# Where the splits of the first weights stand in a planned instruction order, and how long the plan takes conversions to be

## The chip, the cores and the metric

The kernel runs on one core of one Trainium2 chip. The metric is the device time of the whole program in microseconds (us); 1018.32 us is the median of three runs before the change. Five engines matter: TensorE (PE, matrix products; PEld is its weight load), VectorE (DVE), ScalarE (ACT), GpSimd (POOL) and SyncE (SP), which issues all transfers (DMA).

## The reference, in short

2304 tokens (4 batches of 576) pass through three layers in turn:

- attention of 8 heads of 64 columns, masked by blocks of 64 positions: `softmax(q k^T / 8) v`, with the row's maximum taken off before the exponential;
- a first feed-forward layer: `h = x @ w_in`, `g = max(0.01 h, h)`, `y = g @ w_out`, with 512 columns in and out and 2048 between;
- a second one of the same size with `g = h * sigmoid(h)`.

The weights come in as 64-bit floats and are turned into 32-bit floats on the chip.

## The kernel before

**Blocks.** The first two layers run over six blocks of 384 tokens (blocks 0 to 5), the third over nine blocks of 256 tokens. While PE runs the feed-forward steps of block b, the attention of block b+1 runs beside them on DVE, ACT, POOL and in between on PE. One step f (of 16) of a block is a first product with 128 of the 2048 columns (`first_layer`, lines 1114 to 1121), the gate on ACT (L1167), and a second product into four accumulators (`second_layer`, L1131 or L1139). Step (1, 0) is the first step of block 1.

**Precision.** Block 0's feed-forward steps multiply the 32-bit weights as they are (L1114, L1131). All later blocks multiply parts: a weight w is *split* into hi (w rounded to the type that PE takes at full rate) and lo = w - hi. Each half of a step's weights (128 x 512) is one ACT copy (L296) and one subtraction (L312) on DVE or POOL; with 16 steps and two halves each that is 32 copies and 32 subtractions, tile `w` in the trace. Step (1, f) cannot start before its splits are there.

**Conversion.** `convert` turns 128 x 512 weights from 64 to 32 bits: a load, a scaling on ACT (L344), the low word on DVE (L354) or ACT (L352), the sign on DVE (L357), a shift on DVE (L361), and an integer addition on DVE or POOL (L366). It serves the first weights (32 conversions, while block 0 runs) and the second weights (32 conversions, from about 470 us on).

**Where splits go.** The split of the first five steps and of one more half goes into tiles that the start of block 0 leaves; the next ones need the tiles of block 1's keys (free when the last scores of block 1 are done); from the middle of step 8 on they go into the tiles of block 0's own weights.

**Attention.** A unit is 128 queries of a head: scores on PE (L838; L833 for block 1), their maximum on DVE (L847, L850), the exponential on ACT (L855), the normalised probabilities in two parts (L869 or L871, L874), a transposing DMA (L882), and the products with the values on PE (L896 to L898), then two small operations that gather a head's rows (L721, L727). Block 2 has 24 units. When all heads are there, `x` of the block is split in two (tiles xhi, xlo), and the block's first step can start.

**The order.** Nothing is ordered at run time. `Schedule.run` (L84) simulates the engines once, when the program is built: each task has a length per engine that may take it, the tasks it needs, and a rank. An engine that is free takes the waiting task of lowest rank; if a task may go to two engines, the second one is offered it 450 ns later and with the rank raised by 14. What comes out is the order of instructions on each engine, and the chip keeps to it. A length marked `Both` also waits for the port that DVE and POOL share in the plan.

**The ranks.** Gates have rank -1000 and more, scores and value products -500; a step (b, f) of the feed-forward layers has 16 b + f. Conversions of first weights have 10.5 + 0.7 f (10.5 to 21), block 1's attention 11 to 12.6. Block 2's units have 79 to 91.8 in order, and the preparation of their keys and queries stands 4 lower, from 75 on. The splits of step f have `step_of(1, f) - LEAD` and one more for every second half:

```
ts = split(DM, lambda d=d: d["x"], parts, deps, step_of(1, f) - LEAD + i % 2, [last] if last else [])
```

With LEAD = 2.0 that is 14 to 30.

Of the kernel before, what the change touches and what calls it, by code (L numbers as in the profile page):

```python
# [29 lines left out]
LATE = 10  # L30
NATIVE = 15
WARM = 11
LEAD = 2.0
LOAD0 = -1000
TURN = 0
COLD = 1.2
# [176 lines left out]
def attn_mlp_mlp(  # L213
# [13 lines left out]
    NT, DM = out.shape  # L227
# [33 lines left out]
    plan = Schedule()  # L261


    def act(n, psum=False, pointers=0):
        return 0.833 * n + (52 if psum else 94) + 93 * pointers

    def dve(n, pointers=0):
        return Both(1.042 * n + 68 + 61 * pointers)
# [4 lines left out]
    def dve2x(n, pointers=0):  # L273
        return Both(0.521 * n + 68 + 61 * pointers)

    def pool(n):
        return Both(2.35 * n + 100)
# [10 lines left out]
    def dma(deps, rank, size, emit, issue=600, after=()):  # L288
        t = plan.add({"SP": issue}, deps, rank, lambda e: emit(), after)
        done = plan.add({"DMA": size / 360}, [t], rank, lambda e: None)  # L290
        done.issue = t
        return done
# [13 lines left out]
    def on_vector(n):  # L306
        return {"DVE": dve(n), "POOL": pool(n)}
# [9 lines left out]
    def step_of(blk, f):  # L317
        return blk * NF + f
# [7 lines left out]
    def convert(src, f, sl, rk, load_rank, to=None):  # L326

        d = {}  # L330
        raw_free, raw_after, raw_users = raws.next()
        cy_free, cy_after, cy_users = cys.next()
        cc_free, cc_after, cc_users = ccs.next()

        def load():
            r = raw.tile([P, DM], I64, tag="wraw", name="wraw")
            nc.sync.dma_start(out=r, in_=src[f, :, sl])
            d["w0"] = r.bitcast(U32).rearrange("p (n two) -> p n two", two=2)[:, :, 0]
            d["sign"] = r.bitcast(U16).rearrange("p (n four) -> p n four", four=4)[:, :, 3]
            d["top"] = r.bitcast(F32).rearrange("p (n two) -> p n two", two=2)[:, :, 1]  # L340

        def scaled(e):
            d["y"] = cy.tile([P, DM], F32, tag="cy", name="cy")
            nc.scalar.activation(d["y"], d["top"], AF.Copy, scale=2.0**-112)  # L344

        def half_words(i):
            return d["c"].bitcast(U16).rearrange("p (n two) -> p n two", two=2)[:, :, i]

        def low(e):
            d["c"] = cc.tile([P, DM], U32, tag="cc", name="cc")  # L350
            if e == "ACT":
                nc.scalar.activation(half_words(0), d["w0"], AF.Copy, scale=2.0**-29)  # L352
            else:
                nc.vector.tensor_scalar(half_words(0), d["w0"], 2.0**-29, None, op0=ALU.mult)  # L354

        def signed(e):
            nc.vector.tensor_scalar(half_words(1), d["sign"], 0x8000, None, op0=ALU.bitwise_and)  # L357

        def shifted(e):
            yu = d["y"].bitcast(U32)  # L360
            nc.vector.tensor_scalar(yu, yu, 3, None, op0=ALU.logical_shift_left)  # L361

        def added(e):
            ci = d["c"].bitcast(I32)
            d["x"] = d["c"].bitcast(F32) if to is None else to
            engine[e].tensor_tensor(d["x"].bitcast(I32), d["y"].bitcast(I32), ci, op=ALU.add)  # L366

        t_load = dma(raw_free, load_rank, DM * P * 8, load, after=raw_after)
        raws.takers.append(t_load.issue)
        t_y = plan.add({"ACT": act(DM)}, [t_load, *cy_free], rk, scaled, cy_after)  # L370
        cys.takers.append(t_y)
        t_w = plan.add({"DVE": dve2x(DM), "ACT": act(DM)}, [t_load, *cc_free], rk, low, cc_after)
        ccs.takers.append(t_w)
        t_c = plan.add({"DVE": dve2x(DM)}, [t_load], rk, signed, [t_w])
        t_t = plan.add({"DVE": dve2x(DM)}, [t_y], rk, shifted)
        t_x = plan.add(on_vector(DM), [t_w, t_c, t_t], rk, added)
        raw_users += [t_y, t_w, t_c]
        cy_users.append(t_x)
        if to is not None:
            cc_users.append(t_x)  # L380
        return d, t_x, cc_users

    def split(n, value, parts, deps, rk, after=(), on=on_vector):

        hi = plan.add(copy_on(n), deps, rk, lambda e: copy(e, parts()[0], value()), after)
        lo = plan.add(
            on(n), [hi], rk, lambda e: rest(e, parts()[1], value(), parts()[0].bitcast(F32))
        )
        return [hi, lo]

    def first_weights():

        got = []
        for i in range(2 * NF):
            f, sl = i // 2, slice((i % 2) * DM, (i % 2 + 1) * DM)
            rk = CONV0 + CONV1 * f
            to = wx[f][:, sl] if f < NATIVE else None
            got.append(convert(w1, f, sl, rk, LOAD0 + 2 + 10 * i if i < 4 else rk - CONV_LOAD, to))
        return got

    def split_weights():
# [3 lines left out]
        for i in range(2 * NF):  # L405
# [9 lines left out]
            for at in (2 * f, 2 * f + 1):  # L415
# [5 lines left out]
                else:  # L421
                    deps += [steps[j].t_g2, *done[2 * j], *done[2 * j + 1]]
            ts = split(DM, lambda d=d: d["x"], parts, deps, step_of(1, f) - LEAD + i % 2, [last] if last else [])
            last = ts[0]
# [4 lines left out]
    class SecondWeights:  # L429
# [59 lines left out]
        def add_one(self, p, k):  # L489
            rk = pair_of(0, p) - W2_AHEAD  # L490
            f, sl = 2 * p + k % 2, slice(0, DM) if k < 2 else slice(DM, 2 * DM)
            d, t_x, users = convert(w2, f, sl, rk, rk - CONV_LOAD)
            if k < 2 or p >= FAST:
                ts, hi, lo = self.split(DM, lambda: d["x"], [t_x], rk, False)
# [1167 lines left out]
```

## Time and profile before

| | |
|---|---|
| median of three runs | 1018.32 us (1017.8 to 1019.97) |
| the profiled execution | 1017.75 us, its span 1016.0 us |
| PE busy | 981.6 us, 97% of the span |
| DVE busy | 762.7 us, 75% |
| ACT busy | 577.2 us, 57% |
| POOL busy | 196.3 us, 19% |
| granted clock of PE, mean | 0.992 |

PE is nearly always busy, so the time hangs on what PE does and on the few places where it waits. Such a place is found by cutting the span into stages and reading PE's busy time, the granted clock and the busy time of the other engines stage by stage.

### The profile page before, as it was taken

What the parts mean: (1) busy time and instruction counts of PE and PEld (TensorE: products, weight loads), DVE (VectorE), ACT (ScalarE), POOL (GpSimd) and SP (SyncE); (2) the same over time, 40 slices, a digit from 0 to 9 for tenths busy, and PEclk for the clock granted to TensorE, in tenths of its full rate; (3) what the DMA queues carried; (4) which work ended last, traced back from release to release, by engine and by line L of the source; (5) the groups of instructions that cost most, each with busy time, mean ns of one, the idle gap of its engine ahead of it and who ended that gap; (6) DMA issues with size and microseconds to landing.
All of it is one profiled execution on the core that took longest, in us unless ns stands there. A gap on an engine that the chain in (4) does not pass through costs nothing.

```text
span 1016.0 us, 18148 instructions
## 1 busy us (share of the span) xinstructions
PE 981.6 (97%) x6417; PEld 862.8 (85%) x6417; DVE 762.7 (75%) x1891; ACT 577.2 (57%) x1398; POOL 196.3 (19%) x287
## 2 busy tenths in 40 slices
PE   7899999999899999999999999999999999999998
PEld 4656557999799999999999898888989889898897
DVE  6888879687978878877647999976666667666564
ACT  5886768676667666666545668643333333333332
POOL 3173438112130114112203124510000000000000
PEclk9999999999799999999999999999999999999999
DMA  8757772565664656568434445410010100000000
GB/s 266 247 148 179 193 146 71 116 147 111 143 143 117 132 134 123 114 138 191 112 62 135 145 146 176 125 43 22 22 42 1 43 1 22 22 1 22 1 22 22
DMA packets 159451, 102.64 MB, mean 101 GB/s; under 512 B 131456, under 2 KB 143744, under 8 KB 159360
## 3 DMA queue, kind: packets, MB, share of 16 engines
q1 hardware_dynamic: 159360, 101.48, 39.6%
q8 instruction: 50, 0.82, 0.3%
q14 instruction: 41, 0.34, 0.1%
HBM read 67.37 MB, written 9.44 MB: 76 GB/s over the span
## 4 chain that ended last, share of the span: by engine, by line
PE 51%; DVE 3%; DMA 2%; ACT 1%; issue 1%; POOL 0%; SPq 0%; DVEq 0%; POOLq 0%; ACTq 0%
PE h L1332 13%; PE acc L1455 11%; PE acc L1471 7%; PE h L1333 6%; PE acc L1139 6%; PE h L1119 2%; PE h L1121 2%; PE h L1120 2%; PE s L838 1%; DMA wraw<-w 1%; DMA yT<-y 1%; DMA pt<-hl 1%; PE x L896 0%; DMA kqr<-kq_l 0%; PE x L898 0%
## 5 line engine op out<-in xcount | busy, mean ns | idle before, releaser
L1139 PE MATMUL acc<-ghi,w 128*128 128x384 f32 x640 | 164.2, 337 | 1.9 <-ACT ghi L296 1.2
L1344 ACT ACTIVATE xlo<-xlo 128x256 f32<-128x256 f32 x144 | 59.6, 414 | 139.1 <-DVE xlo L1341 139.0
L1332 PE MATMUL h<-xhi,w 128*128 128x512 f32 x352 | 132.0, 398 | 0.0
L1341 DVE TENSOR_REDUCE xlo<-h 128x256 f32<-128x512 f32 x144 | 99.3, 690 | 37.1 <-PE h L1333 34.8
L1139 PEld LDWEIGHTS acc<-ghi,w 128*128 128x128 f32 x640 | 114.0, 188 | 3.3 <-ACT ghi L296 1.5
L1119 PE MATMUL h<-xhi,w 128*128 128x384 f32 x320 | 109.7, 343 | 0.3 <-ACT g L1167 0.3
L1120 PE MATMUL h<-xlo,w 128*128 128x384 f32 x320 | 107.6, 336 | 0.0
L1139 PE MATMUL acc<-glo,w 128*128 128x384 f32 x320 | 107.4, 336 | 0.2 <-DVE glo L312 0.2
L1121 PE MATMUL h<-xhi,w 128*128 128x384 f32 x320 | 107.5, 336 | 0.0
L855 ACT ACTIVATE p<-s,st 128x288 f32<-128x288 f32 (+5 forms) x144 | 73.4, 512 | 47.9 <-DVE st L847 35.2
L1333 PE MATMUL h<-xhi,w 128*128 128x256 f32 x352 | 98.9, 281 | 0.0
L312 DVE TENSOR_TENSOR g<-xlo,xhi 128x256 fp32r<-128x256 f32 x136 | 61.4, 452 | 40.0 <-ACT xhi L296 39.6
L874 DVE SCALAR_TENSOR_TENSOR hl<-p,st,hl 128x576 f16<-128x576 f32 (+6 forms) x120 | 80.4, 674 | 14.5 <-ACT hl L869 11.5
L296 ACT ACTIVATE xhi<-xlo 128x256 fp32r<-128x256 f32 x144 | 59.0, 415 | 48.8 <-PE acc L1455 29.1
L1332 PE MATMUL h<-xlo,w 128*128 128x512 f32 x224 | 85.5, 398 | 0.0
L869 ACT ACTIVATE hl<-p,st 128x576 f16<-128x576 f32 (+7 forms) x111 | 65.8, 596 | 25.9 <-DVE st L865 7.2
L896 PE MATMUL x<-pt,v 128*128 128x128 f16 (+1 forms) x432 | 70.7, 214 | 9.4 <-DMA pt<-hl 4.1
L1332 PEld LDWEIGHTS h<-xhi,w 128*128 128x128 f32 x352 | 66.3, 188 | 13.7
L1167 ACT ACTIVATE g<-h 128x384 f32<-128x384 f32 x96 | 46.6, 485 | 48.1 <-PE h L1121 44.8
L897 PE MATMUL x<-pt,v 128*128 128x128 f16 (+1 forms) x432 | 68.6, 212 | 0.0
L1471 PE MATMUL acc<-w,xhi 128*128 128x512 f32 (+1 forms) x225 | 67.5, 384 | 0.0
L1333 PEld LDWEIGHTS h<-xhi,w 128*128 128x128 f32 x352 | 66.6, 189 | 1.0
(147 smaller groups left out, 2514.4 us busy)
## 6 DMA issues: line engine op xcount, KB each, us to landing
wraw<-w SPq DMA_DIRECT2D x64, 512.0 KB, 4.5
kqr<-kq_l SPq DMA_DIRECT2D x16, 480.0 KB, 4.0
v<-vL SPq DMA_DIRECT2D x32, 160.0 KB, 3.5
out<-o SPq DMA_DIRECT2D x18, 256.0 KB, 2.0
yT<-y SPq DMA_DIRECT2D x20, 192.0 KB, 2.3
kqr<-kq_l SPq DMA_DIRECT2D x8, 416.0 KB, 3.5
kqr<-kq_l SPq DMA_DIRECT2D x8, 384.0 KB, 3.5
yr<-yT SPq DMA_DIRECT2D x6, 512.0 KB, 4.0
```

Source lines behind the costliest of these rows:

```text
L855: nc.scalar.activation(p[:rows, k0:k1], u.s[i][:rows, :w], AF.Exp, bias=nm[:rows], accum_out=s2[:rows, i : i + 1])
L874: nc.vector.scalar_tensor_tensor(hl[:rows, 1, :n], p[:rows], rc[:rows], hl[:rows, 0, :n], op0=ALU.mult, op1=ALU.subtract)
L896: nc.tensor.matmul(g.x[:, o], a, hi, start=j == 0, stop=False)
L1119: nc.tensor.matmul(h, w1_lo[s.f][:, sl], hi[:, c, : s.n], start=c == 0, stop=False)
L1120: nc.tensor.matmul(h, w1_hi[s.f][:, sl], lo[:, c, : s.n], start=False, stop=False)
L1121: nc.tensor.matmul(h, w1_hi[s.f][:, sl], hi[:, c, : s.n], start=False, stop=c == NC - 1)
L1139: nc.tensor.matmul(s.acc[c][:, : s.n], a, b, start=s.f == 0 and i == 0, stop=s.f == NF - 1 and i == 2)
L1332: nc.tensor.matmul(o, whi[:, sl], x, start=c == 0, stop=end, skip_group_check=True)
L1333: nc.tensor.matmul(o[:, :NB2], wlo[:, sl], x[:, :NB2], start=False, stop=end, skip_group_check=True)
L1341: nc.vector.tensor_reduce(place(2 * j, 2), both, axis=AX.X, op=ALU.add)
L1455: nc.tensor.matmul(o, a, b, start=bank not in seen, stop=end and j == 2, skip_group_check=True)
L1471: nc.tensor.matmul(o[:, c], a, b[:, c], start=False, stop=end, skip_group_check=True)
```

## The change

LEAD goes from 2.0 to -55.0, so the splits' ranks go from 14 to 30 up to 71 to 87 (rank 71 + f, and one more for every second half). In `convert`, the lengths that the plan takes for the conversion's operations are raised by 50 to 150 ns. As a side effect of adding a number to them, four lengths on DVE are no longer of the kind `Both`. No instruction is added, removed or altered; what may change is the order on each engine and, where a task may go to two engines, which of them gets it.

```diff
-LEAD = 2.0
+LEAD = -55.0
...
-        t_y = plan.add({"ACT": act(DM)}, [t_load, *cy_free], rk, scaled, cy_after)
+        t_y = plan.add({"ACT": act(DM) + 50}, [t_load, *cy_free], rk, scaled, cy_after)
...
-        t_w = plan.add({"DVE": dve2x(DM), "ACT": act(DM)}, [t_load, *cc_free], rk, low, cc_after)
+        t_w = plan.add({"DVE": dve2x(DM) + 110, "ACT": act(DM) + 150}, [t_load, *cc_free], rk, low, cc_after)
...
-        t_c = plan.add({"DVE": dve2x(DM)}, [t_load], rk, signed, [t_w])
-        t_t = plan.add({"DVE": dve2x(DM)}, [t_y], rk, shifted)
-        t_x = plan.add(on_vector(DM), [t_w, t_c, t_t], rk, added)
+        t_c = plan.add({"DVE": dve2x(DM) + 110}, [t_load], rk, signed, [t_w])
+        t_t = plan.add({"DVE": dve2x(DM) + 60}, [t_y], rk, shifted)
+        t_x = plan.add({"DVE": dve(DM) + 70, "POOL": pool(DM)}, [t_w, t_c, t_t], rk, added)
```

## Rows read from the trace of the kernel before

**Rows 1.** Busy time by stage: stretch, its length, engines (instructions), clock, DMA share, GB/s.
```profile
0.00:50.00 50.00, 38.99 (x199) 25.21 (x199) 37.54 (x114) 33.87 (x93) 12.97 (x22) 0.93 0.77 257
50.00:150.00 100.00, 95.61 (x503) 57.34 (x503) 84.19 (x222) 72.74 (x173) 46.87 (x57) 1.00 0.72 167
150.00:175.00 25.00, 25.00 (x138) 17.59 (x137) 22.01 (x34) 20.36 (x47) 18.26 (x14) 1.00 0.31 87
175.00:190.00 15.00, 15.00 (x103) 14.66 (x103) 9.47 (x25) 9.00 (x23) 4.31 (x9) 1.00 0.30 67
190.00:255.00 65.00, 65.00 (x527) 61.98 (x526) 53.07 (x152) 44.30 (x106) 11.39 (x30) 1.00 0.64 131
255.00:275.00 20.00, 15.35 (x106) 13.21 (x104) 17.97 (x60) 12.36 (x37) 2.72 (x7) 0.74 0.68 138
...
560.00:620.00 60.00, 58.29 (x333) 57.00 (x332) 57.06 (x117) 40.28 (x76) 10.53 (x7) 1.00 0.48 158
620.00:650.00 30.00, 28.52 (x191) 25.89 (x190) 27.03 (x49) 22.36 (x50) 19.50 (x22) 1.00 0.41 133
```

**Rows 2.** Waits of PE, 250 to 310 us: total us, times, longest.
```profile
PE s L838 <- ACT p L855: 2.9, 4, 1.6
PE x L896 <- DMA pt<-hl: 1.6, 3, 0.8
```

**Rows 3.** Timeline of PE, block 1's first step and block 2's: start, length, instruction.
```profile
166.91 0.63 PE L1119 MATMUL h<-xhi,w 128*128 128x384 f32 x1
...
256.97 0.34 PE L1139 MATMUL acc<-glo,w 128*128 128x384 f32 x1
...
267.41 0.33 PE L896 MATMUL x<-pt,v 128*128 128x128 f16 x1
...
271.40 0.67 PE L1119 MATMUL h<-xhi,w 128*128 128x384 f32 x1
```

**Rows 4.** Tile w, 150 to 180 us: ns min/median/max, first and last start.
```profile
L296 ACT ACTIVATE w<-wx x20: 613/621/631, 152.0 to 167.0; 128x512 fp32r<-128x512 f32 x20
L312 DVE TENSOR_TENSOR w<-wx,w x10: 673/693/1782, 152.7 to 167.2; 128x512 fp32r<-128x512 f32 x10
L312 POOL TENSOR_TENSOR w<-wx,w x10: 1269/1719/1784, 156.0 to 170.1; 128x512 fp32r<-128x512 f32 x10
L312 POOL TENSOR_TENSOR w<-cc,w x2: 1284/1288/1292, 173.2 to 175.2; 128x512 fp32r<-128x512 f32 x2
```

**Rows 5.** Timeline, scores on PE and their exponentials on ACT, two early units and a later one.
```profile
155.19 0.54 PE L838 MATMUL s<-k,q 128*128 128x320 f32 x2
...
158.46 0.65 PE L838 MATMUL s<-k,q 128*128 128x448 f32 x2
...
164.32 0.53 ACT L855 ACTIVATE p<-s,st 128x320 f32<-128x320 f32 x1
...
175.92 0.63 ACT L855 ACTIVATE p<-s,st 128x448 f32<-128x448 f32 x1
...
251.28 0.65 PE L838 MATMUL s<-k,q 128*128 128x448 f32 x2
...
253.23 0.64 ACT L855 ACTIVATE p<-s,st 128x448 f32<-128x448 f32 x1 [0.91 <-DVE st L847]
```

**Rows 6.** Tile w, 50 to 80 us.
```profile
L296 ACT ACTIVATE w<-wx x10: 613/616/627, 55.3 to 63.8; 128x512 fp32r<-128x512 f32 x10
L312 POOL TENSOR_TENSOR w<-wx,w x10: 1265/1391/1786, 56.0 to 70.6; 128x512 fp32r<-128x512 f32 x10
```

**Rows 7.** One DVE group by shape, 155 to 177 us, then 190 to 255 us: busy, mean ns.
```profile
L312 DVE TENSOR_TENSOR glo<-g,ghi 128x384 fp32r<-128x384 f32 x2 | 2.9, 1431 | 0.0
...
L312 DVE TENSOR_TENSOR glo<-g,ghi 128x384 fp32r<-128x384 f32 x11 | 6.1, 550 | 0.6 <-ACT ghi L296 0.6
```

**Rows 8.** Conversions by line, 0 to 150 us: ns min/median/max.
```profile
L344 ACT ACTIVATE cy<-wraw x32: 651/674/707, 7.9 to 140.5; 128x512 f32<-128x512 f32 x32
L366 DVE CUSTOM_DVE_ANT_0 wx<-cy,cc x16: 667/678/1441, 16.7 to 134.7; 128x1024 uint16<-128x1024 uint16 x16
```

## The prediction

> **What bounds the kernel now.** I read the stages first. PE is busy in every microsecond of 150 to 255 us and nearly so before and after; the one stretch behind the start where it falls off is 255 to 275 us, with 15.35 of 20 us busy and a granted clock of 0.74 [rows 1]. So it is the work of PE that bounds the kernel, and what an order can change is how long PE waits. I then asked who is waited for there: scores wait for exponentials, value products for the transposing DMA [rows 2]. Both are attention. The timeline of PE says whose attention: block 1's last step ends at 257.3 us, the value products of block 2's last unit start at 267.41, and block 2's first step starts at 271.40 [rows 3]. Between the two steps lie 14 us with nothing of the feed-forward layers: block 2's attention is late. Last I looked for the place where it lost the time. Block 2's first two units have their scores at 155.19 and 158.46 us, but their exponentials at 164.32 and 175.92 [rows 5]; they wait 9.1 and 17.5 us, where a unit of the second one's size waits 2.0 us later on (251.28 to 253.23) [rows 5]. In just that time, from 152.0 on, ACT does twenty of the 32 copies of the splits and two more by 175, DVE and POOL their subtractions [rows 4]. In the plan the splits (14 to 30) stand ahead of the units (79 and up). So the first two units come 7 and 15.5 us late, behind splits of which the last is not used before step (1, 15).
>
> **What the stall is worth.** PE idles 20 - 15.35 = 4.65 us in that stretch [rows 1]. The clock of 0.74 stands for the lower level, 1.2 GHz, in about half of it, after the idle time. What that costs the work that ran: 0.26 x 15.35 = 4.0 us, an estimate, as the low clock is spread over the stretch in it. Together 8.6 us is the most that the stall can give back, and below that some of it stays.
>
> **The change, part by part.**
>
> *The 22 late splits.* Nothing is added or removed: 22 copies at 0.62 us and 22 subtractions, at about 0.69 us on DVE or 1.28 to 1.72 us on POOL [rows 4], are still done, and no DMA moves with them. By rank, six halves (steps 5 to 7, 76 to 79) still go ahead of the first unit or level with it, 6 x 0.62 = 3.7 us of ACT; sixteen (79 to 87) stand among the units. So the second unit's exponential should come near 161 us, some 15 us earlier than 175.92; I take 15 us as the lead that the attention gains at its head. Then the sixteen must be fitted in. ACT hides them: 9.9 us into the 20.7 us that it idles in 190 to 255 us. So can POOL, which is busy 11.4 of those 65 us [rows 1]: 16 x 1.5 = 24 us. On DVE they cost 16 x 0.69 = 11 us of its 11.9 idle us there, which is no cover, as attention needs it. So the lead at the end of block 2's attention lies between 15 - 11 = 4 us (all on DVE, each in front of a unit) and 15 us (all hidden). A second bound is DVE's room: it works 22.0 + 9.5 + 53.1 + 18.0 = 102.5 of the 125 us to 275 [rows 1]; to end 8.6 us earlier it must be 102.5 / 116.4 = 88% busy. It is 90% busy in 255 to 275 [rows 1], so that can be done, but with little over. I take 6.5 us for the stall's loss, near the middle between 4 and 8.6.
>
> *The port.* While POOL did its splits, the same subtraction of 384 columns on DVE took 1431 ns; without them 550 ns [rows 7]. Each DVE operation that meets a POOL split thus loses 0.88 us. Sixteen splits on POOL, if each meets one operation of a unit, cost 14 us of DVE, and that eats the lead: this is a rival below. The Trainium skill, "SBUF — State Buffer", section "Who interferes with whom", says it harder: a DVE instruction with two SBUF inputs and a GpSimd one that reads SBUF take turns at a port pair, and whichever issues second is blocked until the first is through. By that rule sixteen POOL splits take up to 16 x 1.5 = 24 us from DVE, and nothing would be left of the gain; the row agrees as to the direction, at 0.88 us an operation. I weigh it lower because before, too, ten of the twelve splits on POOL ran back to back against DVE, and DVE itself did ten at a stretched pace (worst 1.78 us) [rows 4].
>
> *The ten early splits* (steps 0 to 4), now done at 55 to 71 us [rows 6], get 71 to 76 and give way to conversions and to block 1's attention. They are 6.2 us of ACT and 14 us of POOL, and the stage from 50 to 150 us has 27 and 53 us idle [rows 1], so I cost them at nothing: free engines take waiting work. PE idles 4.4 us in that stage [rows 1]; between nothing and one of them may be won as conversions come sooner. If the cover fails they land at 152 us, ahead of the units, and take 6 us of the lead back.
>
> *The lengths.* The plan had 520 ns for the scaling and 601 for DVE's addition, and gets 570 and 671; the trace shows 674 and 678 [rows 8]. DVE's three other conversion lengths rise as well: 110 + 110 + 60 + 70 = 350 ns per conversion. On the chip no instruction changes, but the order around all 64 conversions is drawn anew, and in the plan four of DVE's operations no longer wait for POOL. The places that this can touch are the start (11 us idle of 50), the stage to 150 us (4.4 idle) and the second weights' stage, 560 to 650 us (3.2 us idle, DVE 84 of 90 us busy) [rows 1]. I have no row that signs it: the bounds are a gain of 2 us (half of the 4.4) and a loss of 4 (the 3.2 idle us doubled, and one more such wait at the start), the value 0.
>
> **The sum.** The profiled execution took 1017.75 us (span 1016.0 and 1.75 around it), 0.57 below the median of 1018.32. 1017.75 - 6.5 = 1011.25; carried over to the median, 1011.8 us. The gain is kept afterwards only if later blocks' attention keeps up; it comes forward with block 2's, and PE waits little for it from 275 us on.
>
> **Rivals.** Changes of less than 0.2% (2 us, here 1016.3 to 1020.4) a measurement of this kernel cannot tell from none.
>
> 1. *The forecast*: the stall shrinks by 4 to 8.6 us, 1009.7 to 1014.3. Chance 0.48.
> 2. *More than the stall*: the lead of up to 15 us also removes waits behind it and about 2 us at the conversions: 1018.3 - 8.6 - 3 = 1006.7. For it: the first units lie open. Against it: DVE would need over 90%. Chance 0.10.
> 3. *The lead is given back*: sixteen splits spread out, DVE stretched by 14 us, no more than 0 to 3 us left, 1015.3 to 1018.3. For it: the 1431 ns [rows 7] and DVE at 82% in 190 to 255 us [rows 1]; also the change might not do what it says, if the plan still finds ACT free at 152 us and sends most splits there in one go. Against it: the units go first whenever both wait. Chance 0.19.
> 4. *Block 1's steps wait for their splits* (slower): from step 9 on a step's splits stand just in front of it, behind a unit, and PE, which takes its steps strictly in turn, waits. Behind it wait all products of PE, scores included. A copy and a subtraction on POOL are 0.62 + 1.5 = 2.1 us [rows 4, 6]; on the seven steps 9 to 15 that is 15 us, less 6.5 gained: 1018.3 + 8.3 = 1026.6. It decides from 6.5 / 7 = 0.9 us per step on. For it: the last half's rank, 87, lies above five eighths of the units. Against it: a step of block 1 comes every 5.6 us (16 in the 90 us from 167 to 257 [rows 3]), and its two halves need 1.2 us of ACT and 3 of POOL. Chance 0.13.
> 5. *The new lengths order the conversions worse* by the 4 us, and 0 to 4 us of the stall is won: 1018.3 to 1022.3. Chance 0.10, half of it beyond 1020.4.
>
> **How the numbers follow.** Faster by over 0.2%: 0.48 + 0.10 + half of the third, 0.09, is 0.67. Within 0.2%: the other 0.10 of the third and 0.05 of the fifth, 0.15. Slower: 0.13 + 0.05 = 0.18. The range holds the first and third case, most of the second and half of the fifth: 1006.5 to 1020.
>
> **What would show it.** Right: in 152 to 176 us fewer than ten copies of tile w on ACT, the second unit's exponential near 161 us; block 2's first step less than 5 us after block 1's last, and a clock of 1.00 in the stage around it. The seventh to last splits at 176 to 250 us, mostly on POOL. Wrong: first products of block 1 (L1119) that wait for tile w on POOL or ACT show case 4; early exponentials with a late first step of block 2 and DVE over 88% busy with stretched operations case 3; more idle PE in 50 to 150 or 560 to 650 us case 5.

## The result, and the profile after

The changed kernel takes 1006.99 us (median of four runs, 1005.73 to 1007.25) against 1019.14 us for the kernel before on the same chip (four runs, 1017.8 to 1021.46): a ratio of 0.9877 [0.9852, 0.9901]. The forecast was 1011.8 us. The sign and the place were right; the gain of 12.15 us is nearly twice the 6.5 us forecast, and the way that leads to it is another one. The time lies 0.5 us inside the stated range (1006.5 to 1020), and outside the forecast's own case (1009.7 to 1014.3).

The profiled execution of after took 1006.94 us, 10.81 less than that of before. The stages of after, in the columns of [rows 1]:

```profile
0.00:50.00 50.00, 39.55 (x210) 25.76 (x211) 39.08 (x119) 36.30 (x98) 12.80 (x23) 0.95 0.76 250
50.00:150.00 100.00, 94.94 (x511) 57.15 (x510) 91.52 (x230) 72.99 (x177) 43.67 (x54) 0.97 0.72 178
150.00:175.00 25.00, 23.86 (x134) 16.30 (x131) 23.05 (x44) 21.11 (x52) 20.33 (x20) 1.00 0.29 63
...
190.00:255.00 65.00, 65.00 (x521) 62.18 (x521) 52.00 (x146) 42.04 (x104) 14.10 (x30) 1.00 0.65 123
255.00:275.00 20.00, 20.00 (x161) 18.95 (x159) 17.81 (x59) 16.59 (x45) 3.51 (x9) 1.00 0.62 151
```

The stall is gone: 255 to 275 us has PE busy throughout at a clock of 1.00, where before had 15.35 us at 0.74. In its place PE idles 1.1 us just behind 150 us, where before idled nothing. PE's timeline, as in [rows 3], shows block 1's first step later than before (171.09 against 166.91) and block 2's sooner (264.68 against 271.40), now right behind block 1's last products:

```profile
171.09 0.42 PE L1119 MATMUL h<-xhi,w 128*128 128x384 f32 x1
...
258.84 0.34 PE L1119 MATMUL h<-xhi,w 128*128 128x384 f32 x1
...
263.76 0.34 PE L1139 MATMUL acc<-glo,w 128*128 128x384 f32 x1
...
264.68 0.39 PE L1119 MATMUL h<-xhi,w 128*128 128x384 f32 x1
...
604.75 0.39 PE L1332 MATMUL h<-xhi,w 128*128 128x512 f32 x1
```

The same cut from the start to block 2's first step, one row of before, one of after, says what the 6.7 us consist of:

```profile
0.00:271.40 271.40, 251.36 (x1552) 186.77 (x1553) 220.81 (x594) 191.10 (x470) 95.65 (x136) 0.97 0.65 161
```
```profile
0.00:264.70 264.70, 248.05 (x1560) 184.47 (x1560) 227.16 (x597) 190.88 (x471) 98.75 (x138) 0.98 0.67 166
```

PE has nearly the same products to do up to that point (after has nine value products more and two scores fewer). It idles 271.40 - 251.36 = 20.0 us before and 16.7 after, 3.4 less; and it is busy 3.3 us less for that work, which goes with the clock, 0.97 against 0.98.

The lead then grows: 6.7 us at block 2's first step, 7.8 at block 5's (538.2 against 546.0), 11.6 at the third layer's first product (604.75 against 616.39), 10.8 at the end. So some 4 us more come while block 5 runs, where PE has no attention left to do. PE's waits there (535 to 620 us) were, in before:

```profile
PE acc L1139 <- ACT ghi L296: 1.2, 1, 1.2
PE acc L1139 <- DVE y L298: 0.7, 1, 0.7
PE h L1119 <- ACT g L1167: 0.3, 1, 0.3
PE acc L1139 <- DVE glo L312: 0.2, 1, 0.2
```

In after PE waits for nothing between 530 us and the third layer. The stage itself, from block 5's first step to the third layer, before and after:

```profile
546.00:616.40 70.40, 68.01 (x386) 66.36 (x385) 61.94 (x124) 44.38 (x86) 13.78 (x10) 1.00 0.48 156
```
```profile
538.00:604.80 66.80, 66.80 (x388) 66.80 (x387) 54.15 (x109) 39.25 (x77) 11.55 (x10) 1.00 0.42 136
```

DVE was 88% busy in it and is now 81%: the last value product (L896) of the attention comes at 513.1 us instead of 529.2, the first sign of a second weight's conversion (L357) starts at 470.1 instead of 479.1, and 16 of these operations instead of 19 are left for the stage. Whether that lead or the second weights' new lengths shorten the stage in after isn't shown: either is enough without the other (e3 and e4 below).

The units got their lead. Scores and exponentials of the first two units and the next two, as in [rows 5]:

```profile
150.27 0.54 PE L838 MATMUL s<-k,q 128*128 128x320 f32 x2
153.53 0.65 PE L838 MATMUL s<-k,q 128*128 128x448 f32 x2
```
```profile
153.58 0.53 ACT L855 ACTIVATE p<-s,st 128x320 f32<-128x320 f32 x1
...
157.84 0.63 ACT L855 ACTIVATE p<-s,st 128x448 f32<-128x448 f32 x1
...
162.50 0.50 ACT L855 ACTIVATE p<-s,st 128x288 f32<-128x288 f32 x1
...
167.77 0.53 ACT L855 ACTIVATE p<-s,st 128x320 f32<-128x320 f32 x1 [3.29 <-DVE st L847]
```

They wait 3.3 and 4.3 us instead of 9.1 and 17.5. But the splits did not move behind them. Tile w, 140 to 190 us, as in [rows 4]:

```profile
L296 ACT ACTIVATE w<-wx x20: 613/620/636, 148.2 to 172.5; 128x512 fp32r<-128x512 f32 x20
L312 POOL TENSOR_TENSOR w<-wx,w x13: 1263/1512/1814, 152.0 to 177.3; 128x512 fp32r<-128x512 f32 x13
L312 DVE TENSOR_TENSOR w<-wx,w x7: 673/686/693, 148.9 to 168.7; 128x512 fp32r<-128x512 f32 x7
```

Twenty copies still fall into 24 us, and the units go between them: by ACT's timeline 7 copies stand ahead of the first unit's exponential (before 16), and 15 ahead of the third one's. The last scores of block 1 (L833) end at 147.0 us instead of 151.9, and block 1's first step starts 4 us later: 24 us lie between the two instead of 15, and splits and units both fit in.

### The profile page after: what moved, and what is told of

It is laid out like the page before. It is cut to its first block, busy times and chain, and to the rows that moved or that the text cites. A ratio compares the mean times of both kernels' runs of the same rounds, so it can differ in the third digit from the quotient of the medians.

```text
span 1005.2 us, 18174 instructions
## 1 busy us (share of the span) xinstructions
PE 975.5 (97%) x6417; PEld 859.1 (85%) x6417; DVE 763.9 (76%) x1899; ACT 576.7 (57%) x1395; POOL 192.9 (19%) x282
## 4 chain that ended last, share of the span: by engine, by line
PE 55%; DVE 4%; DMA 3%; ACT 2%; issue 1%; POOL 0%; SPq 0%; DVEq 0%; ACTq 0%
PE h L1332 13%; PE acc L1455 11%; PE acc L1139 8%; PE acc L1471 7%; PE h L1333 6%; PE h L1119 3%; PE h L1121 3%; PE h L1120 3%; DMA pt<-hl 1%; PE s L838 1%; DMA kqr<-kq_l 1%; PE x L896 1%; DMA wraw<-w 1%; DVE xlo L1341 1%; PE x L898 1%
## 5 line engine op out<-in xcount | busy, mean ns | idle before, releaser
L1119 PE MATMUL h<-xhi,w 128*128 128x384 f32 x320 | 108.6, 340 | 0.0
L874 DVE SCALAR_TENSOR_TENSOR hl<-p,st,hl 128x576 f16<-128x576 f32 (+6 forms) x120 | 86.0, 725 | 14.8 <-ACT hl L869 11.9
L869 ACT ACTIVATE hl<-p,st 128x576 f16<-128x576 f32 (+7 forms) x116 | 68.6, 597 | 26.5 <-DVE st L865 9.1
L896 PE MATMUL x<-pt,v 128*128 128x128 f16 (+1 forms) x432 | 69.1, 211 | 11.4 <-DMA pt<-hl 6.1
L312 DVE TENSOR_TENSOR glo<-g,ghi 128x384 fp32r<-128x384 f32 x80 | 50.7, 634 | 23.1 <-ACT ghi L296 22.3
L1333 PEld LDWEIGHTS h<-xhi,w 128*128 128x128 f32 x352 | 66.6, 189 | 1.8 <-DVE w L312 0.9
```

The costliest lines, as they stand in the source:

```text
L312: engine[e].tensor_tensor(lo, x, hi, op=ALU.subtract)
L874: nc.vector.scalar_tensor_tensor(hl[:rows, 1, :n], p[:rows], rc[:rows], hl[:rows, 0, :n], op0=ALU.mult, op1=ALU.subtract)
L896: nc.tensor.matmul(g.x[:, o], a, hi, start=j == 0, stop=False)
L1119: nc.tensor.matmul(h, w1_lo[s.f][:, sl], hi[:, c, : s.n], start=c == 0, stop=False)
L1333: nc.tensor.matmul(o[:, :NB2], wlo[:, sl], x[:, :NB2], start=False, stop=end, skip_group_check=True)
```

## The experiments

Each was run in five rounds against the kernel before on the same chip. The first four part the change: is it the rank, or the lengths, and of which conversions?

**e1, the rank alone**, on the kernel before.

```diff
-LEAD = 2.0
+LEAD = -55.0
```

> Only the rank of the splits changes (71 to 87), the plan's lengths stay as before. Theory A (two gains: the stall at block 2's first step goes by the rank, about 7 us; the later 4 us, between block 5's first step and the third layer, come from the lengths of the second weights' conversions): 1011 to 1013 us, the 14 us without feed-forward steps before block 2 gone, but about 70 us from block 5's first step to the third layer's first product, as before. Rival B (all of it is the rank: attention that ends some 16 us earlier also starts the second weights earlier): 1006 to 1008 us and 66 to 67 us for that stretch. Rival C (each reordering moves the time by some us at random): anything between 1004 and 1016, with waits at places that neither kernel has.

1020.19 us, ratio 0.9991 [0.9969, 1.0013]: the rank alone gains nothing, which none of the three had allowed for. Scores of block 1 end at 155.0 us, and the copies start at once, for no unit is waiting yet (the first one's scores start at 157.5); 14 of them are through by its exponential:

```profile
L296 ACT ACTIVATE w<-wx x20: 615/620/630, 155.1 to 180.2; 128x512 fp32r<-128x512 f32 x20
```

Two units get through about when block 1's first step starts (166.4 us). The third has its scores at 168.8, its exponential at 184.54, right behind a gate that waited for PE:

```profile
166.61 0.53 ACT L855 ACTIVATE p<-s,st 128x320 f32<-128x320 f32 x1 [0.26 <-DVE st L847]
...
168.73 0.64 ACT L855 ACTIVATE p<-s,st 128x448 f32<-128x448 f32 x1 [0.46 <-DVE st L847]
...
183.59 0.49 ACT L1167 ACTIVATE g<-h 128x384 f32<-128x384 f32 x1 [2.75 <-PE h L1121]
...
184.54 0.49 ACT L855 ACTIVATE p<-s,st 128x288 f32<-128x288 f32 x1
```

The stall is longer: 22.1 us from the start of block 1's last feed-forward product to block 2's first step (before 14.4).

**e2, the lengths alone**, on the kernel after.

```diff
-LEAD = -55.0
+LEAD = 2.0
```

> Only the lengths of the conversions change, the splits keep ranks 14 to 30. Theory A: the stall before block 2 stays (PE idle over 3 us and a lowered clock there), block 5 to the third layer in 66 to 67 us: about 1015 us. Rival B: no gain, 1018 to 1020 us. Rival C: anything between 1008 and 1022.

1023.11 us, 1.0025 [1.0003, 1.0047], above all three ranges. The first exponentials come at 177.71 and 178.49 us, later than before, though block 1's scores end early (148.1): ranked first, the splits take ACT. Neither half is worth anything by itself; the gain is in the two together.

**e3 and e4, the new lengths for the first or the second weights only**, with the new rank. `convert` gets an argument `more` that chooses between the new lengths and the old ones (`Both` with the old); e3:

```diff
-            got.append(convert(w1, f, sl, rk, LOAD0 + 2 + 10 * i if i < 4 else rk - CONV_LOAD, to))
+            got.append(convert(w1, f, sl, rk, LOAD0 + 2 + 10 * i if i < 4 else rk - CONV_LOAD, to, True))
...
-            d, t_x, users = convert(w2, f, sl, rk, rk - CONV_LOAD)
+            d, t_x, users = convert(w2, f, sl, rk, rk - CONV_LOAD, None, False)
```

and e4 the other way round.

> New ranks, new lengths for the first weights' conversions only; the second weights' conversions have the old ones, so the order is that of the changed kernel until they come. Theory A: 1010 to 1012 us, the first lead of 7 to 8 us kept, about 70 us from block 5's first step to the third layer. Rival B: 1006 to 1008 us.

> New ranks, new lengths for the second weights' conversions only. Theory A: the stall goes by the rank and the late 4 us by these lengths: 1006 to 1009 us. Rival B: 1006 to 1008 us too; it differs from theory A only together with the run that has the first weights' lengths. If the first weights' lengths matter for the stall after all, 1011 to 1015 us.

e3: 1005.99 us, 0.9855 [0.9829, 0.9880], the whole gain. e4: 1018.16 us, 0.9976 [0.9959, 0.9993], slower than any of its ranges. So the lengths that count are those of the first weights, drawn up 300 us before the second ones. Block 5 to the third layer takes 66.6 us in e3, as in after, and 67.1 in e4 (e1: 71.0): either the attention's lead or the second weights' new lengths take the waits there away, and together they give no more.

**e5, e6, e7: is it the added nanoseconds or the lost mark `Both`?** e5 keeps the new lengths and puts the mark back:

```diff
-        t_c = plan.add({"DVE": dve2x(DM) + 110}, [t_load], rk, signed, [t_w])
+        t_c = plan.add({"DVE": Both(dve2x(DM) + 110)}, [t_load], rk, signed, [t_w])
```

(the other three alike); e6 keeps the rank and drops the mark, with all additions zero; e7 is e6 with LEAD = 2.0:

```diff
-        t_c = plan.add({"DVE": dve2x(DM) + 110}, [t_load], rk, signed, [t_w])
+        t_c = plan.add({"DVE": dve2x(DM) + 0}, [t_load], rk, signed, [t_w])
```

> The changed kernel (rank 71 to 87, all new lengths), but the four DVE lengths of the conversions stay marked as waiting for the port shared with POOL in the plan. Theory D (the side effect counts: without the mark the plan packs the first weights' conversions closer, block 1's attention ends sooner in the order, and only then can the rank let block 2's units through): the stall before block 2 is back, 1017 to 1025 us, the last scores of block 1 after 150 us. Rival L (the raised nanoseconds count): 1005 to 1009 us, as the changed kernel.

> The new rank and the old lengths, but the DVE lengths of the conversions without the mark of the shared port. Theory D: most of the gain, 1006 to 1012 us, last scores of block 1 before 150 us. Rival L: no gain, 1017 to 1022 us, as the kernel with the new rank alone.

> Old rank (14 to 30) and old lengths; only the mark of the shared port is gone from the conversions' DVE lengths. If the mark alone is enough: 1006 to 1012 us. If rank and mark are both needed (what the run with all new lengths and the old rank suggests, which was no faster than before): 1015 to 1023 us, with block 2's first exponentials behind the splits, after 165 us.

e5: 1025.33 us, 1.0050 [1.0022, 1.0078]. e6: 1020.07, 0.9991 [0.9967, 1.0016]. e7: 1023.40, 1.0019 [0.9993, 1.0044]. With any one of the three left out, rank, added lengths or lost mark, the gain is gone, so theory D and rival L each had half of it. The plan also reads the mark both ways: POOL waits for a marked operation on DVE too (`Schedule.run`).

e5 failed theory D's sign. Block 1's scores end at 142.7 us there, earliest of all, and the stall is the longest (28.9 us from the end of block 1's last feed-forward product, before 14.1). Block 2's first scores come only at 161.0, 18 us behind block 1's last ones (after 3.3), and the second part of the first queries (L670) is made only at 156.68 us, where after makes it at 123.42. The copies start at 143.0, and 16 of the 20 are through before the first unit's exponential (162.50). So an early end of block 1's scores doesn't help a unit that isn't ready by then.

e6 tells most. Its units do get through (exponentials at 162.02, 166.42, 171.48 and 176.35), but its stages show what that cost, in the columns of [rows 1]:

```profile
50.00:150.00 100.00, 90.42 (x462) 53.23 (x463) 86.70 (x226) 69.11 (x164) 33.02 (x42) 0.97 0.69 168
150.00:200.00 50.00, 49.77 (x312) 38.70 (x311) 37.57 (x87) 36.62 (x90) 29.47 (x34) 1.00 0.41 92
```

PE idles 9.6 us from 50 to 150, block 1's scores end at 156.5 and its first step comes at 176.4.

**e8 and e9: is it the rank as such?** After, with splits further behind or two ranks later.

```diff
-LEAD = -55.0
+LEAD = -80.0
```

> The changed kernel with LEAD -80: the splits' ranks are 96 to 112, behind all units of block 2. If the gain comes from the splits giving way to block 2's units, this does at least as well: 1003 to 1009 us, unless block 1's steps wait for their splits (L1119 behind tile w). If the gain hangs on the one order that rank 71 to 87 happens to give, it is lost in part: 1010 to 1018 us.

and e9 with `LEAD = -57.0`.

> The changed kernel with LEAD -57: the splits stand two ranks lower (73 to 89), still among block 2's units, all else as changed. If a rank among the units is what gains, 1005 to 1009 us. Rival C (the gain hangs on the one order that LEAD -55 gives): 1010 to 1018 us, with a stretch of over 5 us without feed-forward products before block 2's first step.

e8: 1016.93 us, 0.9963 [0.9938, 0.9987]. e9: 1010.02 us, 0.9904 [0.9875, 0.9933]. Both fall where the gain was to hang on the one order that rank 71 to 87 gives, e9 with a stretch of 8.6 us in front of block 2's first step. A rank behind every unit keeps a third of the gain, not more of it. In e9 a part of the stall is back: PE is busy 21.74 of the 25 us from 255 to 280 (before 20.35, after 24.71).

**e10 and e12: the work of the splits, or their place?** Both leave out the 32 subtractions of the splits, so that lo equals hi, and keep the order of everything else: e10 that of before, e12 that of e1. (A line was added, so line numbers are one higher; the lines that hand `skip` on and put hi in place of lo are not shown.)

```diff
-            on(n), [hi], rk, lambda e: rest(e, parts()[1], value(), parts()[0].bitcast(F32))
+            on(n), [hi], rk, lambda e: None if skip else rest(e, parts()[1], value(), parts()[0].bitcast(F32))
```

> The kernel before, in its order, but the 32 subtractions of the first weights' splits are left out (lo is not computed; PE reads hi in its place), the copies stay and the plan still counts the subtractions' time. Theory P (the work of the subtractions on DVE and POOL, and the port that POOL's take from DVE, is what holds block 2's attention back): the stall before block 2 shrinks from 14.4 to under 5 us, 1008 to 1013 us. Rival Q (it is the place in the queues: the copies on ACT and the gates that wait for PE): the stall stays over 9 us, 1015 to 1019 us.

> The kernel with the new rank alone (LEAD -55, old lengths; it was no faster than before), in its order, without the 32 subtractions as in the run beside it. Theory P: its stall of 22 us goes down to under 8 us, 1006 to 1013 us; what kept the rank from helping is that the subtractions then fall on DVE and POOL together with block 2's first units and block 1's first steps. Rival Q: the stall stays over 15 us, 1015 to 1020 us.

e10: 1018.93 us, 0.9993 [0.9971, 1.0015]. e12: 1020.40 us, 1.0005 [0.9983, 1.0028]. The stages of before, then of e10:

```profile
150.00:200.00 50.00, 50.00 (x315) 41.76 (x314) 39.67 (x83) 35.65 (x83) 24.28 (x28) 1.00 0.41 97
255.00:280.00 25.00, 20.35 (x152) 18.05 (x151) 22.48 (x77) 17.31 (x51) 3.84 (x9) 0.80 0.71 148
```
```profile
150.00:200.00 50.00, 50.00 (x312) 41.64 (x311) 23.98 (x73) 35.54 (x84) 5.10 (x15) 1.00 0.42 96
255.00:280.00 25.00, 20.68 (x161) 18.30 (x159) 22.79 (x77) 17.42 (x50) 4.54 (x10) 0.80 0.66 145
```

DVE loses 15.7 us of work, POOL 19.2, and the stall stays as it was (14.0 us in e10, before 14.1; 22.0 in e12, e1 21.7). So it is not that DVE is full; what is left is the order in which the units stand, and the copies on ACT, which both runs keep. What the second unit waits for is first its maximum on DVE, before and then in e10:

```profile
170.75 1.52 DVE L312 TENSOR_TENSOR glo<-g,ghi 128x384 fp32r<-128x384 f32 x1
...
175.02 0.62 DVE L847 TENSOR_REDUCE st<-s 128x1 f32<-128x448 f32 x1
```
```profile
171.46 0.56 DVE L312 TENSOR_TENSOR glo<-g,ghi 128x384 fp32r<-128x384 f32 x1 [3.74 <-ACT ghi L296]
...
173.25 0.62 DVE L848 TENSOR_REDUCE st<-s 128x1 f32<-128x448 f32 x1
```

Its scores start at 158.46 and 159.32 us. In e10 DVE even stands idle for 3.74 us, with that maximum behind an operation of block 1's first step (`glo`, the low part of the gate's result) that waits for ACT, whose gate waited for PE. In after the maximum comes at 155.74, ahead of that step. ACT's wait for PE's steps (145 to 200 us), in before, e10 and after:

```profile
ACT g L1167 <- PE h L1121: 7.7, 5, 2.8
```
```profile
ACT g L1168 <- PE h L1122: 7.8, 5, 2.8
```
```profile
ACT g L1167 <- PE h L1121: 2.1, 3, 0.9
```

Once block 1's steps run, gates stand in ACT's queue, and an exponential behind one waits for PE's step, as the third unit's does in e1. What goes ahead of block 1's first step escapes that. That the head of a queue, DVE's and ACT's, holds the units is read from these rows; no run moved a gate alone, and none left out the copies.

**e11, the mark gone from all lengths.**

```diff
-        return Both(1.042 * n + 68 + 61 * pointers)
+        return float(1.042 * n + 68 + 61 * pointers)
```

(two more alike)

> The changed kernel, and the mark of the shared port is gone from every length in the plan, not only the conversions'. If the mark makes the plan worse wherever it stands: at least as fast as the changed kernel, 1001 to 1007 us. If it is right elsewhere (POOL's operations do hold up DVE's on the chip): 1009 to 1020 us, with more PE waits for DVE in the attention stages.

1028.40 us, 1.0081 [1.0049, 1.0112], slower than either range. The lost mark is no gain in itself: PE idles 10.8 us from 50 to 150 us, and block 1 starts at 184.9.

**All together.** PE's idle time by stage (length less busy time, from the stages' view) up to block 2's first step:

| kernel | ratio | block 1 starts | block 2 starts | idle 0 to 50 | 50 to 150 | 150 to block 2 | sum |
|---|---|---|---|---|---|---|---|
| before | 1 | 166.9 | 271.4 | 11.0 | 4.4 | 4.7 | 20.0 |
| after | 0.9877 | 171.1 | 264.7 | 10.5 | 5.1 | 1.1 | 16.7 |
| e1 rank | 0.9991 | 166.4 | 277.7 | 11.1 | 1.6 | 9.4 | 22.1 |
| e2 lengths | 1.0025 | 168.2 | 277.9 | 9.0 | 6.8 | 6.4 | 22.2 |
| e3 first lengths | 0.9855 | 169.9 | 263.6 | 9.1 | 5.6 | 1.2 | 15.8 |
| e4 second lengths | 0.9976 | 165.5 | 276.8 | 11.7 | 3.2 | 9.2 | 24.1 |
| e5 mark kept | 1.0050 | 161.6 | 278.8 | 7.8 | 1.2 | 14.5 | 23.5 |
| e6 rank, no mark | 0.9991 | 176.4 | 275.0 | 10.1 | 9.6 | 3.0 | 22.7 |
| e7 no mark | 1.0019 | 176.6 | 273.2 | 10.2 | 8.1 | 1.5 | 19.7 |
| e8 LEAD -80 | 0.9963 | 171.2 | 273.5 | 8.1 | 5.5 | 6.2 | 19.8 |
| e9 LEAD -57 | 0.9904 | 169.6 | 268.0 | 9.0 | 5.6 | 3.3 | 17.8 |
| e11 no mark at all | 1.0081 | 184.9 | 283.6 | 9.5 | 10.8 | 5.6 | 25.9 |

An order that starts block 1 early (e1, e4, e5) pays at block 2, one that starts it late (e6, e7, e11) pays ahead of 150 us. After, e3 and e9 have the lowest sums and are the three fastest; between e3 and after the ratios don't decide, as their intervals overlap. Among the others the sum doesn't order the times: e4 idles 24.1 us and is 0.24% faster than before, e7 idles 19.7 us and is no faster. What comes behind block 2's first step counts too: from there to block 5's first step e4 takes 270.9 us and e7 278.3 (before 274.6).

## Why the prediction was right or wrong, step by step

- **The stall at block 2's first step bounds this stage, and goes: right.** The forecast of 6.5 us there met 6.7. That it comes so near is luck: the 6.5 were worked out for the rank, with the lengths at 0, and the rank alone leaves a longer stall (e1). The estimate that idle time and low clock share the loss about evenly (4.65 and 4.0) holds for what was won, 3.4 and 3.3.
- **The units come sooner: right.** The second unit's exponential was put near 161 us and came at 157.84. Of these 18 us, 4.9 come from its scores, which start at 153.53 instead of 158.46, as block 1's end sooner; the prediction had no such term. Nor was it the copies on ACT alone that held this unit before: its maximum stood on DVE until 175.02.
- **Because most splits move behind the units, to 176 to 250 us: wrong.** Its sign, fewer than ten copies in 152 to 176 us, failed: ACT's timeline has 15 in that time. The new rank lets waiting units pass; it doesn't hold back splits for which ACT is free. With the rank alone most copies ran while no unit was ready (e1), the objection that stood beside the third rival.
- **The lengths, put at 0 between a gain of 2 us and a loss of 4: this is the step that failed.** With the new rank, the first weights' lengths are worth 14 us (e1 1020.19, e3 1005.99); with the old one nothing or a loss (e2). I took the lengths as something that could add waits or not at the conversions, and cost the rank by itself. In fact they move the end of block 1's scores and the start of its first step, and with that how many units get through between the two: 24 us lie there in after and in e3, 11 in e1. That this gap is what lets the rank act is read from the timelines; it isn't enough by itself, since the units must be ready (e5, 19 us). With the old rank e7 has 23 us there and a stall of only 3.8, but pays for it with a first step at 176.6.
- **The ten early splits at no cost: right as far as the runs show.** They ran at 48.6 to 68.2 us. With the rank alone PE idles 1.6 us from 50 to 150 us, less than the 4.4 before; after idles 5.1 there, at a clock of 0.97, with the new lengths too.
- **The rival of spread splits and stretched DVE operations: wrong in mechanism.** While POOL subtracts, DVE's operation is slow, 1431 ns against 550 [rows 7], but taking all 32 subtractions away bought nothing (e10, e12). The Trainium skill, "SBUF — State Buffer", section "Who interferes with whom", has a DVE instruction with two SBUF inputs contend with a GpSimd one that reads SBUF. The stretched operations agree with it; as a price in the kernel's time it is 0 within 0.3% in the orders of before and e1, where leaving the subtractions out leaves the stall. That DVE did its ten splits "at a stretched pace" was read too strongly: their median of 693 ns [rows 4] is that of after's seven, 686 ns.
- **Block 1's steps waiting for their splits: did not happen**; no wait of L1119 for tile w shows in after.
- **"More than the stall" (1006.7, chance 0.10) came nearest in time.** Its reason held in part: a lead that goes on paying behind the stall, but in block 5, not at the first conversions; there the attention's earlier end and the second weights' new lengths each do nearly as much alone (e3, e4). "PE waits little for it from 275 us on" overlooked the 2.4 us that PE waited at 554 to 566 us.

What stays open: why this set of lengths, with the mark gone, ends block 1's scores at 147 us with the units ready behind them, when with the same rank e6 needs 156.5 and e8, with the same lengths, 156.0, and e5 ends them at 142.7 with no unit ready. The orders differ at many places between 50 and 150 us, and no run changed one alone. Nor was it tried to hold splits back by anything other than the rank.

## What to carry to other kernels

Where a plan fixes the order on every engine, a rank and a length act together: try each by itself before saying which one gained, and expect a near value (LEAD -57, 0.9904) to give another time. Read the gain as PE's idle time in each stage up to the next block's start; a stage that improves while an earlier one pays is no gain. And to tell work from order, leave the work out and keep the order: if the time stays, look at what stands in front in the queue.

## What the runs showed of the hardware that was not expected

Work taken from an engine that is 79% busy right where the units run (DVE, 39.67 to 23.98 of 50 us) left the time as it was. And idle time of PE cost about as much again by the clock: after saves 3.4 us of it up to block 2's first step and 3.3 us of busy time. In e12 the 25 us from 255 to 280 have PE busy for 18.13 us at a granted clock of 0.66 on average, so the products around the waits ran in large part at the lower level, 1.2 GHz.
